# Conv-GLU behind windowed attention: the first chunk's feed-forward in float32, weights split later, and another order for the opening

## The chip, the core and the metric

The kernel runs on one core of a Trainium2 chip. The metric is the device time of one execution in microseconds (us). PE is TensorE, DVE VectorE, ACT ScalarE, POOL GpSimd, SP SyncE, whose queue issues all DMAs here.

## The reference

Eight batches of 576 positions, eight heads of 64, float32; the weights arrive as float64 (512 x 1024, 3 x 1024, 1024 x 512).

```python
scores = q @ k.T / sqrt(64)
scores = where((rel >= 0) & (rel < 128), scores - slopes[h] * abs(rel), -1e9)   # rel = query - key
attn = exp(scores - max(scores)); attn = attn / (sum(attn) + 1e-9)
x = (attn @ v)                                  # heads side by side: (8, 576, 512)
h = maximum(x @ w_in, 0)
conv = sum(conv_w[k] * h shifted by k - 1, k = 0, 1, 2)     # along positions, zero outside a batch
out = (h * sigmoid(conv)) @ w_out
```

## The kernel before

The 4608 tokens are taken in 36 tiles of 128, numbered t, and in 18 chunks of two tiles. A step s is one chunk and one pair of the eight 128-wide feature blocks f; four steps make a chunk.

Attention, for each tile and each half u of four heads: q and k are loaded (`LD`), transposed on PE (`Q`, L272) and copied out by ACT (`QO`, L276). `S` (L303) multiplies them into two PSUM banks, a = 0 and 1, each with two heads. Only 128 columns of a tile's window are live for each row: the merge `MA` puts the part of the previous tile into place with a predicated copy (L321) and then writes -1/8 of the scores plus the bias to SBUF (L334). `RM` takes the minimum (L338), `X` is exp on ACT, one instruction a head, with the row sum accumulated (L343), `N` adds 1e-9, takes reciprocals and scales on DVE (L354 to L356), `T` transposes on PE (L363), `RL` copies out on ACT (L368), `SEL` splits the two tiles' parts on GpSimd (L374, L377), and `AV` multiplies with v in float32 (L393). Scores of tiles below 9 are one float32 pass; later ones are three float32r passes on high and low parts.

The feed-forward works on high and low parts in float32r. `XH` (L404) rounds x on ACT into `ring`, `XL` (L408) subtracts on DVE. `UH` (L440) makes one feature block from 12 matmuls: four of 128 rows deep, three products each (high by high, high by low, low by high). `HH` is Relu on ACT, `Z` and `CV` the convolution (ACT into PSUM, then DVE, L472), `TH` tanh, `GT` the gate (L485), `GH` (ACT, L495) and `GL` (GpSimd, L500) its high and low part, `D` the down-projection (L517, again three products), `OB` the store. The first chunk's up-projections have 258 columns, later ones 256.

The weights come in 16 blocks of 128 x 512 doubles and one of conv weights, through six staging buffers: fetch `F` (SP), clamp `CL` (GpSimd), rebias `RS` (ACT), sign `SG` (GpSimd) or shift `SH` (DVE), bits `V` (two DVE passes, L181 and L188). `H` rounds the high half on ACT (L195). For the low half, `P` subtracts on PE: identity times the float32 weight (L206), then minus identity times the high half (L207), and `W` copies it out on ACT (L216); blocks 6, 14, 15, 16 are subtracted on DVE and block 9 on GpSimd instead (L214).

The order of all engines' instructions is written out by hand: `OPENING` for tiles 0 to 5 and steps 0 to 5, then `PERIOD` once for each tile from `FIRST` = 6 on, with its two steps, then `TAIL`. Each engine takes its instructions in that order. Names in it are as above, followed by tile, half and part, or by the step; a piece whose condition doesn't hold (a tile's `XF`, say) issues nothing. PSUM has five banks with the tag `tr` (transposes, scores, AV, up-projections), one for the convolution and two with the tag `o` for the output.

Of the kernel before, what the change touches and what calls it, by code (L numbers as in the profile page):

```python
# [646 lines left out]
```

## Time and profile before

| | |
|---|---|
| median of 3 runs | 650.45 us (648.82 to 651.15) |
| profiled execution, its own time | 651.56 us |
| its span, first to last instruction | 649.8 us |
| PE, PE weight loads | 628.3 us (97%), 551.2 us (85%) |
| DVE, ACT, GpSimd | 548.7 us (84%), 434.8 us (67%), 211.3 us (33%) |

Busy times are of one profiled execution. Matmuls overlap and their ends are modelled, so PE's busy time includes latency; a float32 matmul that is no transpose appears as two records. On DVE and ACT a record can end after the next has begun: what an instruction costs its engine is the step from its start to the next start.

### The profile page before, as it was taken

To read this page: it belongs to the slowest core of one execution; us is meant where nothing else is said; L and a number is where in the kernel's file an instruction comes from. 1 tells how busy PE (TensorE), PEld (TensorE's weight loads), DVE (VectorE), ACT (ScalarE), POOL (GpSimd) and SP (SyncE) were. 2 spreads that over 40 slices of the span, in tenths; PEclk is the share of its full clock that TensorE was granted. 3 is DMA by queue.
4 is the path that set the end of the run, shared out by engine and by line. 5 is a ranking of instruction groups with operands and counts; after the bars stand their busy time and mean duration, and the time that the engine had idled before them with its cause. 6 is when DMAs were issued, how large, how long until landed. Compare 5 with 4: busy or idle time off the path is not lost.

```text
span 649.8 us, 13737 instructions
## 1 busy us (share of the span) xinstructions
PE 628.3 (97%) x5082; PEld 551.2 (85%) x5082; DVE 548.7 (84%) x1227; ACT 434.8 (67%) x1204; POOL 211.3 (33%) x321
## 2 busy tenths in 40 slices
PE   5789999999999999999999999999999999999997
PEld 4358788888999899998899999999899989998985
DVE  6979997788888899898888898889888889899553
ACT  4868786666766576767676667666676657666653
POOL 3244633332232333333233332222223223333321
PEclk9889999999999999999999999999999999999999
DMA  8876043232323222222402232323232323000001
GB/s 242 220 187 177 21 97 82 50 83 49 83 49 83 49 67 45 74 40 73 96 34 50 65 66 51 80 49 82 50 82 49 83 49 83 18 34 1 33 16 50
DMA packets 120102, 47.04 MB, mean 72 GB/s; under 512 B 113356, under 2 KB 113380, under 8 KB 120036
## 3 DMA queue, kind: packets, MB, share of 16 engines
q1 hardware_dynamic: 120036, 46.17, 29.3%
q8 instruction: 40, 0.66, 0.4%
q14 instruction: 26, 0.21, 0.1%
HBM read 36.72 MB, written 9.44 MB: 71 GB/s over the span
## 4 chain that ended last, share of the span: by engine, by line
PE 83%; DVE 13%; issue 2%; DMA 1%; ACT 1%; POOL 0%; SPq 0%; DVEq 0%; ACTq 0%; POOLq 0%
PE p L440 30%; PE o L517 29%; PE av L393 8%; PE sc L303 8%; PE pt L272 4%; PE pa L363 4%; DVE zp L472 2%; DVE sc L321 2%; DVE wg L188 1%; DVE e L334 1%; DVE wst L181 1%; DVE st L338 1%; DVE ring L408 1%; DVE e L356 1%; DVE z L485 1%
## 5 line engine op out<-in xcount | busy, mean ns | idle before, releaser
L440 PE MATMUL p<-ring,wi 128*128 128x256 f32 (+1 forms) x1728 | 220.8, 284 | 1.5 <-DVE ring L413 1.1
L440 PEld LDWEIGHTS p<-ring,wi 128*128 128x128 f32 x1728 | 211.9, 189 | 7.6 <-PE o L517 2.4
L472 DVE SCALAR_TENSOR_TENSOR zp<-hh,cw,zp 128x256 f32<-128x256 f32 (+7 forms) x384 | 161.9, 422 | 33.5 <-ACT zp L459 22.6
L517 PE MATMUL o<-wo,gh 128*128 128x512 f32 x576 | 186.5, 404 | 0.0
L343 ACT ACTIVATE e<-e,st 128x128 f32<-128x128 f32 x288 | 112.3, 392 | 97.3 <-DVE st L338 97.3
L500 POOL TENSOR_TENSOR gl<-z,gh 128x512 fp32r<-128x512 f32 x71 | 91.3, 1286 | 193.8 <-ACT gh L495 172.8
L517 PEld LDWEIGHTS o<-wo,gh 128*128 128x128 f32 x576 | 103.2, 188 | 25.9 <-issue 5.0
L517 PE MATMUL o<-wo,gl 128*128 128x512 f32 x288 | 114.1, 396 | 0.3 <-POOL gl L500 0.3
L374 POOL TENSOR_SCALAR_AFFINE_SELECT rl<-rl 128x512 f32<-128x512 f32 x64 | 41.4, 646 | 169.9 <-ACT rl L368 166.5
L459 ACT ACTIVATE zp<-hh,cw 128x256 f32<-128x256 f32 x144 | 68.9, 479 | 20.4 <-DVE z L485 14.8
L485 DVE SCALAR_TENSOR_TENSOR z<-zp,hh 128x512 f32<-128x512 f32 (+1 forms) x73 | 49.8, 683 | 36.2 <-ACT zp L480 35.2
L480 ACT ACTIVATE zp<-zp 128x512 f32<-128x512 f32 (+1 forms) x73 | 42.3, 579 | 42.8 <-DVE zp L472 40.0
L393 PE MATMUL av<-rl,rv 128*64 128x128 f32 x1088 | 67.2, 276 | 1.2 <-PE pa L363 0.7
L517 PEld LDWEIGHTS o<-wo,gl 128*128 128x128 f32 x288 | 54.1, 188 | 13.5 <-POOL gl L500 0.7
L334 DVE SCALAR_TENSOR_TENSOR e<-sc,bias 128x256 f32<-128x256 f32 x144 | 61.2, 425 | 5.1
L393 PEld LDWEIGHTS av<-rl,rv 128*64 128x64 f32 x1088 | 58.7, 137 | 6.9 <-issue 2.8
L303 PE MATMUL sc<-qkT 64*128 64x256 f32 (+1 forms) x360 | 55.2, 357 | 1.4 <-DVE e L334 1.2
L321 DVE COPY_PREDICATED sc<-m_prev,sc 128x256 f32<-128x256 uint8 x128 | 53.8, 420 | 2.7 <-PE sc L303 2.7
L377 POOL TENSOR_SCALAR_AFFINE_SELECT rl<-rl 128x512 f32<-128x512 f32 x72 | 45.7, 635 | 30.2 <-ACT rl L368 24.6
L343 ACT ACTIVATION_READ_ACCUMULATOR e<-e,st 128x1 f32 x288 | 54.1, 188 | 0.0
L356 DVE TENSOR_TENSOR e<-e,st 128x512 f32<-128x512 f32 x72 | 50.7, 704 | 2.5
L338 DVE TENSOR_REDUCE st<-e 128x4 f32<-128x512 f32 x72 | 49.2, 685 | 2.1
(76 smaller groups left out, 745.4 us busy)
## 6 DMA issues: line engine op xcount, KB each, us to landing
out_dram<-ob SPq DMA_DIRECT2D x36, 256.0 KB, 2.2
rqk<-in_q_dram SPq DMA_DIRECT2D x32, 256.0 KB, 4.1
rqk<-in_k_dram SPq DMA_DIRECT2D x32, 256.0 KB, 4.3
rv<-in_v_dram SPq DMA_DIRECT2D x32, 256.0 KB, 3.3
wst<-in_moe_w_in_dram SPq DMA_DIRECT2D x8, 512.0 KB, 6.1
wst<-in_moe_w_out_dram SPq DMA_DIRECT2D x8, 512.0 KB, 4.1
rqk<-in_q_dram SPq DMA_DIRECT2D x8, 128.0 KB, 3.6
rqk<-in_k_dram SPq DMA_DIRECT2D x8, 128.0 KB, 3.4
```

The lines of the kernel that those rows point to most:

```text
L303: nc.tensor.matmul(to, tq[rows, slot, u, 0, g, :], of, start=n == 0, stop=n == len(passes) - 1)
L321: nc.vector.copy_predicated(out=s_cur, mask=mask.unsqueeze(1).to_broadcast(shp), data=data)
L334: nc.vector.scalar_tensor_tensor(out=heads, in0=s_cur, scalar=-0.125, in1=b, op0=ALU.mult, op1=ALU.add)
L343: nc.scalar.activation(out=e[:, j, :], in_=e[:, j, :], func=AF.Exp, bias=st[:, 0, j : j + 1], scale=-1.0, accum_out=st[:, 1, j : j + 1],)
L356: nc.vector.tensor_tensor(out=e, in0=e, in1=st[:, 2, :].unsqueeze(2).to_broadcast([P, HU, P]), op=ALU.mult)
L393: nc.tensor.matmul(ps[a * D : (a + 1) * D, u * NG + g], vraw[tt][:, u * HU + j], rl[:, side, j], start=n == 0, stop=n == len(sides) - 1,)
L440: nc.tensor.matmul(ps, a[:, cc, f * P : (f + 1) * P], ring[:, i, cc, cols], start=n == 0, stop=n == last)
L459: nc.scalar.activation(out=zps[s][:, ff, :], in_=hhs[s][:, ff, 1 : 1 + CW], func=AF.Copy, scale=cw[:, 1, f : f + 1])
L472: nc.vector.scalar_tensor_tensor(out=z[:, ff, a:cut], in0=hh[:, ff, a + kk : cut + kk], scalar=cw[:, kk, f : f + 1], in1=z[:, ff, a:cut], ...
L485: nc.vector.scalar_tensor_tensor(out=zgs[s][:, ff], in0=zps[s][:, ff], scalar=1.0, in1=hhs[s][:, ff, 1 : 1 + CW], op0=ALU.add, op1=ALU.mult,)
L500: nc.gpsimd.tensor_tensor(out=gl, in0=zgs.pop(s), in1=as32(gh), op=ALU.subtract)
L517: nc.tensor.matmul(oos[c][m], g[:, ff, ms], w[:, f, :], start=f == 0 and n == 0, stop=f == NFC - 1 and n == 2)
```

## The change

- The first chunk's up- and down-projections (steps 0 to 3) are float32, one product a matmul, on the float32 weights (`wgs`) and on `x_first`, an unsplit copy of x; they have no `GH`, and `GL` only moves the convolution's two border columns. `XL` of tiles 0 and 1 falls away.
- The low halves of all weights are subtracted on GpSimd (11 blocks) or DVE (5), written later in the order; `P` remains for the conv weights alone. The float32 weights and the low halves share 18 buffers. Seven rebias passes go to GpSimd (`RP`). Five blocks more are taken with a shift on DVE instead of a sign pass on GpSimd.
- For tiles 0 to 5 (`EARLY`), q is scaled by -1/8 in `QV`, the bias is added on PE by one float32r matmul with the identity for each bank, the merge only places and masks, the minimum is taken per bank from PSUM, and exp reads PSUM. Tiles 0 to 2 put the scores of half 0 into the output's banks. Reciprocals are taken for a tile at once (`NR`). Ten of these twelve halves are scaled on ACT (`NA`, four instructions), two on DVE.
- `OPENING` is a new order. It holds tiles 0 to 7 and steps 0 to 9, loads tile 0 in halves (`LH`), and `FIRST` is 8. `PERIOD` and `TAIL` are as before.

```diff
-    wst, wgs, pws = {}, {}, {}
-    SIGNS = {0, 1, 2, 3, 5, 6, 7, 8, 9, 10, 11, 12, 13, 14, 15, 16}
-    LOW_POOL = {9}
-    LOW_DVE = {6, 14, 15, 16}
+    wst, wgs, pws, wls = {}, {}, {}, {}
+    NWL = 18
+    SIGNS = {0, 1, 2, 8, 9, 10, 11, 12, 13, 15, 16}
+    LOW_POOL = {0, 1, 5, 6, 7, 8, 9, 13, 14, 15, 16}
...
-    def w_rebias(b):
-        g = wpool.tile([P, WB], U32, name=f"wg{b}", tag="wg")
-        wgs[b] = g[:NW, :P] if blocks[b] is None else g
-        nc.scalar.activation(out=wgs[b].bitcast(F32), in_=wst[b][..., 1].bitcast(F32), func=AF.Copy, scale=2.0**-112)
-
+    def w_rebias(b, pool=False):
+        if b in wgs:
+            pass
+        elif blocks[b] is None:
+            wgs[b] = cpool.tile([P, P], U32, name="wgc")[:NW]
+        else:
+            wgs[b] = wpool.tile([P, WB], U32, name=f"wg{b}", tag="wl", bufs=NWL)
+        g, hf = wgs[b].bitcast(F32), wst[b][..., 1].bitcast(F32)
+        if pool:
+            nc.gpsimd.tensor_scalar(out=g, in0=hf, scalar1=2.0**-112, scalar2=1.0, op0=ALU.mult, op1=ALU.mult)
+        else:
+            nc.scalar.activation(out=g, in_=hf, func=AF.Copy, scale=2.0**-112)
...
     def w_rest(b):
+        ps = pws[b] = pst.tile([P, NW], F32, name="pcw", tag="tr")
+        nc.tensor.transpose(ps, wgs[b].bitcast(F32), ident[:NW, :NW])
+
+    def w_lo(b):
         f = wgs[b].bitcast(F32)
         if blocks[b] is None:
-            ps = pws[b] = pst.tile([P, NW], F32, name="pcw", tag="tr")
-            nc.tensor.transpose(ps, f, ident[:NW, :NW])
+            nc.scalar.copy(out=cw.rearrange("p k f -> p (k f)"), in_=pws.pop(b))
             return
-        if b in LOW_POOL or b in LOW_DVE:
-            return
-        ps = pws[b] = pst.tile([P, WB], F32, name=f"pw{b}", tag="tr")
-        nc.tensor.matmul(ps, ident, f, start=True, stop=False)
-        nc.tensor.matmul(ps, nident, blocks[b][1][0], start=False, stop=True)
-
-    def w_lo(b):
-        out = cw.rearrange("p k f -> p (k f)") if blocks[b] is None else blocks[b][1][1]
-        f = wgs.pop(b).bitcast(F32)
-        if b in LOW_POOL or b in LOW_DVE:
-            eng = nc.gpsimd if b in LOW_POOL else nc.vector
-            eng.tensor_tensor(out=out, in0=f, in1=as32(blocks[b][1][0]), op=ALU.subtract)
-        else:
-            nc.scalar.copy(out=out, in_=pws.pop(b))
-
-
-
+        wls[b] = wpool.tile([P, WB], F32R, name=f"wl{b}", tag="wl", bufs=NWL)
+        eng = nc.gpsimd if b in LOW_POOL else nc.vector
+        eng.tensor_tensor(out=wls[b], in0=f, in1=as32(blocks[b][1]), op=ALU.subtract)
...
+    def load_half(t, u):
+        if t not in raws:
+            raws[t] = [apool.tile([P, 2, H, D], F32, name=f"rqk{t}", tag="rqk", bufs=3)]
+        heads = slice(u * HU, (u + 1) * HU)
+        for i, src in enumerate((q, k)):
+            fetch(t, raws[t][0][:, i, heads], src[:, heads])
...
-        nc.scalar.copy(out=qkT_of(t)[:, t % SLOTS, u], in_=pts.pop((t, u)) if t < SPLIT else pts[t, u])
+        to = qkT_of(t)[:, t % SLOTS, u]
+        if t < EARLY:
+            ps = pts.pop((t, u))
+            nc.scalar.activation(out=to[:, 0], in_=ps[:, 0], func=AF.Copy, scale=-0.125)
+            nc.scalar.copy(out=to[:, 1], in_=ps[:, 1])
+        else:
+            nc.scalar.copy(out=to, in_=pts.pop((t, u)) if t < SPLIT else pts[t, u])
...
-        pss = [pst.tile([P, NG, 2, P], F32, name=f"sc{t}_{u}_{a}", tag="tr") for a in range(2)]
+        if t < 3 and u == 0:
+            pss = [pso.tile([P, NG, 2, P], F32, name=f"sc{t}_{u}_{a}", tag="o") for a in range(2)]
+        else:
+            pss = [pst.tile([P, NG, 2, P], F32, name=f"sc{t}_{u}_{a}", tag="tr") for a in range(2)]
+        if t < EARLY:
+            for a in range(2):
+                b = heads_of(bias_r[:, u * HU : (u + 1) * HU], a)
+                to = pss[a] if first else pss[a][:, :, cur]
+                b = b.unsqueeze(2).to_broadcast([P, NG, 2, P]) if first else b
+                nc.tensor.matmul(to, ident_r, b, start=True, stop=False)
...
-                        to, tq[rows, slot, u, 0, g, :], of, start=n == 0, stop=n == len(passes) - 1
+                        to, tq[rows, slot, u, 0, g, :], of, start=n == 0 and t >= EARLY,
+                        stop=n == len(passes) - 1 and (t >= EARLY or g == NG - 1),
...
-        negb = neg.unsqueeze(2).to_broadcast(shp)
+        negb = (pos if t < EARLY else neg).unsqueeze(2).to_broadcast(shp)
...
+        if t < EARLY:
+            return
...
-    def rowmax(t, u):
+    def rowmax(t, u, a=None):
         e, st, pss = sms[t, u]
+        if t < EARLY:
+            cur = window(t)[-1]
+            least = st[:, 0].rearrange("p (g a) -> p a g", a=2)[:, a]
+            nc.vector.tensor_reduce(out=least, in_=pss[a][:, :, cur, :], axis=mybir.AxisListType.X, op=ALU.min)
+            return
         nc.vector.tensor_reduce(out=st[:, 0, :], in_=e, axis=mybir.AxisListType.X, op=ALU.min)
...
-                in_=e[:, j, :],
+                in_=pss[j % 2][:, j // 2, cur, :] if t < EARLY else e[:, j, :],
...
+    def recips(t, u=None):
+        st = sts.pop(t) if t < EARLY else sms[t, u][1]
         nc.vector.tensor_scalar(out=st[:, 2, :], in0=st[:, 1, :], scalar1=1e-9, scalar2=None, op0=ALU.add)
         nc.vector.reciprocal(out=st[:, 2, :], in_=st[:, 2, :])
+
+    def normal(t, u):
...
+    def normal_act(t, u):
+        e, st, pss = sms[t, u]
+        for j in range(HU):
+            nc.scalar.activation(out=e[:, j, :], in_=e[:, j, :], func=AF.Copy, scale=st[:, 2, j : j + 1])
         es[t, u] = e
...
+        if t < CT:
+            nc.scalar.copy(out=x_first[:, :, 1 + t * P : 1 + (t + 1) * P], in_=avs.pop(t)[0])
+            return
+        if t == CT:
+            nc.scalar.copy(out=x_first[:, :, 1 + CW : 2 + CW], in_=ps[:, :, 0:1])
...
     def x_lo(t):
+        if t < CT:
+            return
...
+            b, part = in_block(cc, f)
+            if s < NFP:
                 nc.tensor.matmul(
-                    ps, a[:, cc, f * P : (f + 1) * P], ring[:, i, cc, cols], start=n == 0, stop=n == last
+                    ps, wgs[b].bitcast(F32)[:, part], x_first[:, cc], start=cc == 0, stop=cc == NCC - 1
                 )
-                n += 1
+                continue
+            for n, (a, i) in enumerate(((blocks[b][1], 0), (blocks[b][1], 1), (wls[b], 0))):
+                nc.tensor.matmul(
+                    ps, a[:, part], ring[:, i, cc, cols], start=cc == 0 and n == 0, stop=cc == NCC - 1 and n == 2
+                )
...
+            if s < NFP:
+                zgs[s] = fpool.tile([P, 2, CW], F32, name=f"z{s}", tag="gh", bufs=3)
...
     def g_hi(s, ff=slice(0, 2)):
+        if s < NFP:
+            return
...
     def g_lo(s, ff=None):
+        if s < NFP:
+            nc.gpsimd.tensor_copy(out=hhs[s][:, :, 0:2], in_=hhs[s][:, :, CW : CW + 2])
+            return
...
+            b = out_block(f)
+            if s < NFP:
                 nc.tensor.matmul(
-                    oos[c][m], g[:, ff, ms], w[:, f, :], start=f == 0 and n == 0, stop=f == NFC - 1 and n == 2
+                    oos[c][m], g[:, ff, ms], wgs[b].bitcast(F32), start=f == 0, stop=f == NFC - 1
+                )
+                continue
+            for n, (a, w) in enumerate(((gh, blocks[b][1]), (gh, wls[b]), (gl, blocks[b][1]))):
+                nc.tensor.matmul(
...
     OPENING = """
-    LD0 Q0 F1 QO0 S0.0 CL1 RS1 S0.1 MA0.0.0 MA0.1.1 LD1 F2 SG1 Q1 MA0.1.0 V1 QO1 S1.0 F0 MA0.0.1 MA1.0.1 LD2
-    CL2 CL0 RM0.0 S1.1 RS2 RS0 F7 H1 F3 X0.0.0 SG2 F5 X0.0.1 MA1.1.1 SG0 LV0 Q2 MA1.0.0 F4 P1 QO2 V0 F9
-    RM0.1 S2.1 F8 N0.0 LD3 W1 X0.1.1 V2 MA1.1.0 MA2.1.1 T0.0 X0.1.0 RL0.0 H0 SEL0.0 P0 RM1.1 H2 S2.0 W0 CL3
...
+    LH0.1 QU0.1 QV0.1 LH0.0 QU0.0 QV0.0 LD1 F4 S0.1 F2 CL4 MA0.1.0 CL2 RM0.1.0 S0.0 RS4 XF3 QU1.1 MA0.0.1
+    MA0.1.1 QU1.0 X0.1.0 MA0.0.0 QV1.1 RP2 RM0.0.0 LD2 F5 RM0.1.1 SG2 RM0.0.1 S1.1 F6 GH0 MA1.1.0 CL5 F0
+    QU2.1 V2 QU2.0 CL6 QV1.0 LD3 RM1.1.0 X0.0.0 F1 MA1.1.1 X0.0.1 RM1.1.1 S1.0 X0.1.1 QV2.1 X1.1.0 NR0 N0.0
+    GH2 F7 MA1.0.1 S2.1 RP6 LD4 RM1.0.1 MA2.1.0 QV2.0 MA1.0.0 X1.1.1 NA0.1 X1.0.1 RM1.0.0 RM2.1.0 T0.0 LV0
+    X1.0.0 SH4 CL0 T0.1 V4 NR1 S2.0 RL0.1 QU3.0 MA2.1.1 F3 N1.0 SH5 SEL0.1 RM2.1.1 X2.1.0 QL7 MA2.0.0 NA1.1
+    RL0.0 RM2.0.0 CL1 XF0 OB4 QU3.1 QV3.0 MA2.0.1 RP0 LD5 S3.0 RM2.0.1 MA3.0.1 RP1 CL7 SG0 QV3.1 SH7 F8 LV1
+    T1.1 X2.1.1 MA3.0.0 RM3.0.1 S3.1 MA3.1.0 LV2 P4 X2.0.0 RL1.1 RM3.0.0 X2.0.1 X3.0.1 MA3.1.1 RS7 RP5 T1.0
...
+    D0 XH4 H8 Z2.0 W1 H11 W0 T5.1 GT1 GL0 W3 OB5 LV6 QV7.0 SG12 S7.0 XL4 HH2.1 RS16 NA5.0 W7 HH3.1 RL5.1 XL3
+    XF2 XF4 S7.1 W2 CV2.0 RM6.0 MA7.0.0 Z2.1 T5.0 UH4.0 W8 UH4.1 X6.0.0 H9 CV2.1 RP13 TH2 UH5.0 GL1 MA7.1.0
...
-    FIRST = 6
+    FIRST = 8
```

## Rows read from the trace of the kernel before

**Rows 1.** The page: PE's busy tenths in 40 slices of the span

```profile
PE   5789999999999999999999999999999999999997
```

**Rows 2.** Windows: us, busy PE, loads, DVE, ACT, POOL; clock, DMA share, GB/s

```profile
0.00:55.56 55.56, 40.92 (x259) 26.99 (x259) 45.42 (x114) 37.23 (x107) 20.74 (x39) 0.91 0.79 209
8.37:55.56 47.19, 37.53 (x243) 24.30 (x241) 42.23 (x93) 34.78 (x104) 19.19 (x30) 0.89 0.80 214
55.56:135.23 79.67, 78.14 (x589) 67.08 (x587) 69.24 (x140) 59.19 (x161) 33.86 (x49) 1.00 0.31 73
```

**Rows 3.** Chain that ended last, 100 to 136 us: start, us, what, records

```profile
101.07 1.93 PE sc L303 x16
103.00 1.90 PE av L393 x32
...
107.89 4.29 PE p L440 x36
112.17 0.87 PE pt L272 x8
...
114.91 2.80 PE o L517 x12
...
135.23 0.84 PE sc L303 x5
```

**Rows 4.** The same chain from 0 to 120 us

```profile
1.30 4.30 DMA rqk<-in_k_dram
...
18.61 0.09 DVE st L354
18.72 0.19 DVE st L355
18.93 0.69 DVE e L356
...
20.95 0.35 DVE sc L321
21.32 0.42 DVE e L334
...
22.61 0.59 DVE st L338
...
38.66 0.93 PE pw L206 x2
39.58 0.23 PE pw L207
```

**Rows 5.** Timeline of ACT: start, us, line, instruction

```profile
59.90 0.38 ACT L449 ACTIVATE hh<-p 128x258 f32<-128x258 f32 x1
60.18 0.39 ACT L343 ACTIVATE e<-e,st 128x128 f32<-128x128 f32 x1
60.47 0.19 ACT L343 ACTIVATION_READ_ACCUMULATOR e<-e,st 128x1 f32 x1
60.56 0.39 ACT L343 ACTIVATE e<-e,st 128x128 f32<-128x128 f32 x1
...
60.95 0.57 ACT L368 COPY rl<-pa 128x512 f32<-128x512 f32 x1
61.41 0.67 ACT L166 ACTIVATE wg<-wst 128x512 f32<-128x512 f32 x1
```

**Rows 6.** Groups on GpSimd, first 115 us: count | busy us, mean ns | idle

```profile
L500 POOL TENSOR_TENSOR gl<-z,gh 128x512 fp32r<-128x512 f32 x6 | 7.9, 1316 | 14.0 <-ACT gh L495 11.4 <-DVE wo L214 2.6
...
L214 POOL TENSOR_TENSOR wo<-wg,wo 128x512 fp32r<-128x512 f32 x1 | 1.7, 1723 | 0.0
```

**Rows 7.** Timeline of GpSimd and DVE at 51.7 us

```profile
51.69 0.68 POOL L171 TENSOR_SCALAR wst<-wst 128x512 f32<-128x512 f32 x1
51.87 1.04 DVE L356 TENSOR_TENSOR e<-e,st 128x512 f32<-128x512 f32 x1
```

**Rows 8.** The page, costliest groups: weight loads of the up-projection

```profile
L440 PEld LDWEIGHTS p<-ring,wi 128*128 128x128 f32 x1728 | 211.9, 189 | 7.6 <-PE o L517 2.4
```

More of the change, by code (lines that the diff above doesn't have):

```diff
@@ L70, in tile_alibi_window_attention_conv_glu @@
     nc.vector.memset(neg, NEG)
+    pos = cpool.tile([P, 1], F32, name="pos")
+    nc.vector.memset(pos, -0.125 * NEG)
     def mask_from(name, conds):
@@ L107, in tile_alibi_window_attention_conv_glu @@
     )
-    bias = cpool.tile([P, H, P], F32, name="bias")
+    EARLY = 6
+    bias_r = cpool.tile([P, H, P], F32R, name="bias")
+    bias = as32(bias_r)
     for h in range(H):
@@ L111, in tile_alibi_window_attention_conv_glu @@
         nc.vector.tensor_scalar(
-            out=bias[:, h, :], in0=dist, scalar1=slope, scalar2=None, op0=ALU.mult
+            out=bias_r[:, h, :], in0=dist, scalar1=slope, scalar2=None, op0=ALU.mult
         )
-    wi = [cpool.tile([P, NCC, DFF], F32R, name=f"wi{i}") for i in range(2)]
-    wo = [cpool.tile([P, NFC, DM], F32R, name=f"wo{i}") for i in range(2)]
+    wi = cpool.tile([P, NCC, DFF], F32R, name="wi")
+    wo = cpool.tile([P, NFC, DM], F32R, name="wo")
     cw = cpool.tile([P, 3, NFC], F32, name="cw")
@@ L131, in weight_blocks @@
             for c in range(NCC):
-                yield moe_w_in[c * P : (c + 1) * P, cols], [w[:, c, cols] for w in wi]
+                yield moe_w_in[c * P : (c + 1) * P, cols], wi[:, c, cols]
             if part == 0:
@@ L135, in weight_blocks @@
         for f in range(NFC):
-            yield moe_w_out[f * P : (f + 1) * P, :], [w[:, f, :] for w in wo]
+            yield moe_w_out[f * P : (f + 1) * P, :], wo[:, f, :]
     wpool = ctx.enter_context(tc.tile_pool(name="wpool", bufs=3))
@@ L235, in tile_alibi_window_attention_conv_glu @@
     ring = cpool.tile([P, 2, NCC, RING + 4], F32R, name="ring")
-    nc.vector.memset(as32(ring[:, :, :, 2:3]), 0.0)
+    x_first = cpool.tile([P, NCC, XW], F32, name="x_first")
+    nc.vector.memset(x_first[:, :, 0:1], 0.0)
     def window_x(c):
-        if c == 0:
-            return slice(2, 2 + XW)
         a = 4 + c * CW % RING
@@ L312, in merge @@
             e = apool.tile([P, HU, P], F32, name=f"e{t}_{u}", tag="e", bufs=4)
-            st = apool.tile([P, 3, HU], F32, name=f"st{t}_{u}", tag="st", bufs=5)
+            if t >= EARLY:
+                st = apool.tile([P, 3, HU], F32, name=f"st{t}_{u}", tag="st", bufs=5)
+            else:
+                if t not in sts:
+                    sts[t] = apool.tile([P, 3, H], F32, name=f"st{t}", tag="sts", bufs=2)
+                st = sts[t][:, :, u * HU : (u + 1) * HU]
             sms[t, u] = e, st, sms[t, u]
@@ L431, in up @@
             ps = pts[s, ff, "up"] = pst.tile([P, 512], F32, name=f"p{s}_{ff}", tag="tr")
-            ps = ps[:, : cols.stop - cols.start]
+            ps = ps[:, : XW if s < NFP else CW]
         else:
@@ L483, in gate @@
         if s not in zgs:
-            zgs[s] = fpool.tile([P, 2, CW], F32, name=f"z{s}", tag="z", bufs=2)
+            if s < NFP:
+                zgs[s] = fpool.tile([P, 2, CW], F32, name=f"z{s}", tag="gh", bufs=3)
+            else:
+                zgs[s] = fpool.tile([P, 2, CW], F32, name=f"z{s}", tag="z", bufs=2)
         nc.vector.scalar_tensor_tensor(
@@ L515, in down @@
             ms = slice(m * P, (m + 1) * P)
-            for n, (g, w) in enumerate(((gh, wo[0]), (gh, wo[1]), (gl, wo[0]))):
+            b = out_block(f)
+            if s < NFP:
                 nc.tensor.matmul(
-                    oos[c][m], g[:, ff, ms], w[:, f, :], start=f == 0 and n == 0, stop=f == NFC - 1 and n == 2
+                    oos[c][m], g[:, ff, ms], wgs[b].bitcast(F32), start=f == 0, stop=f == NFC - 1
[3 more added lines that the diff above has]
+                nc.tensor.matmul(
+                    oos[c][m], a[:, ff, ms], w, start=f == 0 and n == 0, stop=f == NFC - 1 and n == 2
                 )
@@ L549, in tile_alibi_window_attention_conv_glu @@
     TILE = {
-        "LD": load, "LV": loadv, "Q": qk, "QO": qk_out, "QL": qk_rest, "S": scores, "MA": merge, "RM": rowmax,
-        "X": lambda t, u, h: exps(t, u, range(2 * h, 2 * h + 2)),
-        "N": normal, "T": attnT, "RL": attn_out, "SEL": select, "AV": av, "XH": x_hi, "XL": x_lo, "XF": xfin,
+        "LD": load, "LH": load_half, "QU": qkT, "QV": qkT_out, "LV": loadv, "Q": qk, "QO": qk_out, "QL": qk_rest, "S": scores, "MA": merge, "RM": rowmax,
+        "X": lambda t, u, h: exps(t, u, range(h, HU, 2) if t < EARLY else range(2 * h, 2 * h + 2)),
+        "NR": recips, "N": normal, "NA": normal_act, "T": attnT, "RL": attn_out, "SEL": select, "AV": av, "XH": x_hi, "XL": x_lo, "XF": xfin,
     }
@@ L596, in tile_alibi_window_attention_conv_glu @@
+    V16 GH4 RL7.0 LD9 AV5 SEL6.1 SEL7.0 CV5.1 GH1 TH5 GT5 H12 AV6 XH6 D3 XH5 W9 HH6 W12 GH5 XL5 Z6.0 XL6 H13
+    UH8.0 CV6.0 Z6.1 CV6.1 OB3 H14 TH6 GL5 Z7.0 GT6 GL4 UH9.0 W13 CV7.0 XL1 OB6 W10 H16 UH8.1 X7.1.1 W11 GH6
+    Z7.1 N7.1 LV7 GL6 W16 D4 W14 CV7.1 TH7 HH8 Z8.0 H4 GT7 LD10 GH7 CV8.0 D5 Z8.1 D6 UH9.1 GL7 HH9 CV8.1 TH8
+    T7.1 W15 GT8 Z9.0 RL7.1 SEL7.1 LV8 GH8 GL8 D7 CV9.0 Z9.1 OB7 CV9.1 TH9 GT9
     """
```

63 lines of the change are left out of this document (35 added, 28 removed).

## Prediction

> **What bounds the kernel now.** Read the 40 slices first: TensorE (PE) is busy nine tenths or more from the fourth of them on, less in the first three [rows 1]. But a busy PE is not a dense one. The chain that ended last says where PE sets the time: from 101.07 us on it is PE, instruction behind instruction, two tiles in the 34.16 us to 135.23 [rows 3]. Before that the chain runs through VectorE (DVE) [rows 4]. [...] So a change to the opening is worth what it brings forward in PE's work, and nothing after it is changed: at 135.23 PE starts the scores of tile 8, the same instructions follow in both programs, with Q8, AV6, D7 and UH9 issued before it in both. I forecast the start of tile 8's scores, T8.
>
> **PE's own work up to T8.** Costs are steps from start to start. From [rows 3]: an up unit (12 float32r matmuls of 256 columns) 4.29 / 3 = 1.43; a down unit (12 of 512) 2.80; AV 1.90; eight transposes 0.87; a float32 score half of four matmuls 0.97 (half of 1.93). From [rows 4]: a float32 matmul of 512 columns, written as two records, 0.93; the float32r one behind it 0.23. In the order before, up to tile 8: nine transposed tiles 7.8, 16 halves of scores 14.5 (tile 0 at half price), 11 weight splits of 0.93 + 0.23 = 12.8, one of 0.2 for the conv weights, 16 probability transposes 7.0, AV 12.4 (tile 0 half), 20 up units 28.6, 8 down units 22.4: 105.7 of 135.2. Thirty us are lost, 26 of them before the first up-projection (30.0 of work in 55.56).
>
> The change takes the 11 splits away (-12.8). It adds 20 bias matmuls of 512 columns and 4 of 256: 20 x 0.233 + 4 x 0.119 = +5.1. A float32 up unit is 4 matmuls at four times 0.119: 1.91, eight of them +3.8. A float32 down unit is 4 x 0.93 = 3.72, four of them +3.7. Sum -0.2: PE's work stays 105.5. [...]
>
> **DVE**, 45.4 + 69.2 = 114.7 busy to T8 [rows 2]. Merge without bias: -24 x 0.42 = -10.1; ten scalings go to ACT: -10 x 0.69 = -6.9; reciprocals for a tile at once: -6 x (0.11 + 0.21) = -1.9; 12 minima over 512 (0.59) become 24 over 256 from PSUM, 0.30 to 0.42, taken at 0.38 (near the 0.35 to 0.42 of a PSUM pass of that width): +2.0; two fewer remainders of x: -1.4 [all rows 4]. Five shifts more, not in the trace at that width: above 0.35 (a pass of half the width), at most 0.69, taken at 0.4 as they have one input: +2.0; one low half more: +0.7. Sum -15.6: 99.
>
> **ACT**, 37.2 + 59.2 = 96.4 [rows 2]. An instruction is followed by the next some 0.1 before it ends [rows 5]. Gone: 11 copies of low halves (0.47), 7 rebias passes (0.67 less 0.1), 4 roundings of the gate (0.5): -5.2 - 4.0 - 2.0. New: 40 scalings of 128 columns. The exp of that shape steps 0.29 before its accumulator read; a 258-column Relu steps 0.28, so a plain one may be 0.19. I take 0.29, the same shape with a pointer operand: +11.6 (low end +7.6). Copies of q and k in two halves of 256 columns, 0.28 each for 0.48: 12 x 0.08 = +1.0. Sum +1.4: 98. The exps now read PSUM, at the same price here. [...]
>
> **GpSimd**, 54.6 [rows 2]: ten subtractions more at 1.32 to 1.72 [rows 6], +15; 7 rebias passes and 5 fewer sign passes at 0.68 [rows 7], +1.4; four fewer gate remainders, -5.3: 66. Not the bound.
>
> **DMA.** Same bytes; the weights still go through six buffers, and SyncE's (SP) queue holds tile 4's and 5's loads behind weights 7 and 3, which wait for a staging buffer that a DVE pass on an earlier weight frees; both are among DVE's first 12 us of work, and those tiles' transposes are over 25 us in. The opening's first transfers, half the heads of q and k, are half of the bytes that had landed by 5.60 [rows 4]; the first transposes move up by about a us, and I put ACT's first copy at 4.5.
>
> **Waits that are added.** Sixteen weights and their low halves share 18 buffers, so the third low half waits for a weight that the first chunk has done with. Behind it on DVE stand the second chunk's passes, on GpSimd the selections of tile 5; the up-projections that free the buffer stand ahead of the waiting passes by 5 us and more of PE's work, so I cost it at nothing; if that cover is gone, the second chunk's first up-projection is late by what is missing. The wait for score banks is rival 3.
>
> **First stage, to the first up-projection.** Written ahead of it in the new order: on ACT 12 copies of q and k halves (6.7), 4 rebias passes (2.0), 40 exps at 0.39 (15.6), 24 scalings (7.0), 8 copies of probabilities (3.9), x (1.7): 37.0. On DVE, 3.2 of constants and 20 merges (10.1), 20 minima (7.6), seven weights (8.7), the rest 5.6: 35.2 instead of 45.4. On PE 28.0: 12 half transposes 5.2, 11 halves of scores 9.7 and their bias 4.7, 8 probability transposes 3.5, AV 4.8, 0.2. So ACT leads where DVE led. From 4.5, 37.0 at the 89% at which DVE worked gives 46. Its floor is 41.5; with the low price for the scalings, 43. I take 45.5, since part of the doubt is on that side; up to 52 if three engines of nearly the same load wait for each other.
>
> **Second stage.** PE has 105.5 - 28.0 = 77.5 left, ACT 61, DVE 64. Before, PE lost 3.9 here (75.8 of work in 79.7). With DVE lighter I take 3, between 1 and 8. T8 = 45.5 + 77.5 + 3 = 126.0 against 135.23: 9.2 us earlier. The profiled execution took 651.56, which is 1.1 above the median of the runs: 642.4, and for a median **641**.
>
> **Rivals.**
> (1) *The engines interlock nearly without waiting.* ACT at its floor, 41.5, and 1 lost afterwards: T8 = 120, **635**. For it: four engines have slack. Against it: with ACT 37, DVE 35 and PE 28 at a clock that was 0.89 [rows 2] no engine clearly leads, and each wait is passed on.
> (2) *GpSimd blocks DVE.* In [rows 7] a DVE multiply of two SBUF tensors took 1.04 instead of 0.69 because a GpSimd pass of 0.68 had begun 0.18 before it. Ten subtractions of 1.32 or more, nearly all after the first up-projection, could each hold such a DVE pass (weights, scaling, remainders) for their whole length: 13 us, DVE 77 of some 80, at 89% that is 86. T8 = 45.5 + 86 = 132, **647**. Against it: most DVE work of that stage, conv, has one operand in PSUM. [...]
> (3) *No change: PSUM banks.* Exps read the scores where they lie, so a half of scores holds two banks until its last exp, not until its merge: at least 1.4 + 4 x 0.38 + 4 x 0.39 = 4.5 us against some 2.6. Five banks also serve transposes; the first three tiles borrow the output's two. The eight other halves before the up-projection, two at a time, take 48 us once a half holds its banks for 12. From the first scores at 6 the first stage then ends at about 55: T8 = 135.5, **651**.
> (4) *Slower: float32 matmuls that show their weight loads.* One load is 0.189 [rows 8]; 48 float32 matmuls have two each. If none were hidden, +18: T8 = 144, **659**. The gain is gone once half of them show. Against it: AV is float32 with two loads a matmul, and its 32 records run back to back at 59 ns [rows 3].
>
> **Chances and range.** Forecast 0.52, (1) 0.17, (2) 0.15, (3) 0.10, (4) 0.06. A difference under 0.5% can hardly be told from none; faster than 647.2 are the forecast but for 0.03, all of (1) and half of (2): 0.74; same 0.17 (the other half, most of (3), the 0.03); slower 0.09. The range 631 to 650 leaves out (4), two thirds of (3) and the far end of (1).
>
> **What would show it.** First up-projection near 45 us with ACT at nine tenths ahead of it; T8 near 126; no L206; up records in the first chunk at twice the columns, a float32 unit near 1.9, a down unit near 3.7; the row minimum near 0.38 and ACT's scaling near 0.29 a step; all after T8 as before. Wrong if the opening's PE rows wait on exps for banks, if DVE passes beside GpSimd subtractions stretch past a microsecond in number, or if a later stage changes.

## The result, and the profile after

The changed kernel takes 639.77 us (median of four runs, 638.63 to 640.18). The kernel before, run beside it, took 650.2, and the ratio is 0.9838, 95% interval 0.9816 to 0.9861. The prediction was 641, range 631 to 650. The profiled execution took 639.5 us with a span of 637.4.

The windows of the changed kernel, cut at the first up-projection and at the start of tile 8's scores (us, busy PE, loads, DVE, ACT, POOL, granted clock, DMA share, GB/s), answer to [rows 2]:

```profile
0.00:46.13 46.13, 38.75 (x272) 26.08 (x273) 35.58 (x98) 36.93 (x145) 21.13 (x36) 0.96 0.98 235
46.13:125.04 78.91, 77.14 (x516) 61.09 (x515) 66.72 (x128) 57.14 (x154) 46.68 (x59) 1.00 0.34 84
125.04:637.40 512.36, 506.58 (x4241) 456.68 (x4240) 433.43 (x973) 337.91 (x938) 157.12 (x234) 1.00 0.25 58
```

The span is 12.4 us shorter. Of that, 9.43 lies ahead of the first up-projection (55.56 before, 46.13 now), 0.76 between there and tile 8's scores (79.67, now 78.91), and 2.21 behind them, where both programs are the same: 649.80 - 135.23 = 514.57 before, 512.36 now. ACT and DVE have nearly the same work in the first stage, the DMA share there is 0.98 where it was 0.79, and the mean granted clock 0.96 where it was 0.91. The 12.4 is the difference of two single executions; the medians differ by 10.4, since the profiled execution of the kernel before was slower than its median and the changed kernel's was not.

The page's busy tenths for PE [rows 1 has them before]:

```profile
PE   7899999999999999999999999999999999999997
```

PE is below nine tenths in the first two slices, where it was in the first three.

The chain that ended last, from the first up-projection to tile 8's scores (start, us, what, records), answers to [rows 3]:

```profile
46.13 1.76 PE p L505 x8
...
87.21 3.44 PE o L596 x8
...
119.53 1.29 POOL gl L577
...
120.95 1.24 POOL wl L217
...
122.23 2.81 PE o L601 x11
125.04 1.06 PE sc L336 x7
```

A float32 up unit (the first row) is 1.76 us and a float32 down unit 3.44. At the end of the stage TensorE waits for two GpSimd subtractions, the second of them a weight's low half.

### The profile page after: what moved, and what is told of

It is laid out like the page before. It is cut to its first block, busy times and chain, and to the rows that moved or that the text cites. A ratio compares the mean times of both kernels' runs of the same rounds, so it can differ in the third digit from the quotient of the medians.

```text
span 637.4 us, 13650 instructions
## 1 busy us (share of the span) xinstructions
PE 622.5 (98%) x5025; PEld 543.8 (85%) x5025; DVE 535.7 (84%) x1197; ACT 432.0 (68%) x1235; POOL 224.9 (35%) x329
## 4 chain that ended last, share of the span: by engine, by line
PE 77%; DVE 11%; ACT 6%; issue 2%; DMA 2%; SPq 1%; POOL 1%; DVEq 0%; ACTq 0%; POOLq 0%
PE p L510 27%; PE o L601 24%; PE av L451 8%; PE sc L336 7%; PE pa L421 4%; DVE zp L541 4%; PE pt L285 4%; DMA rqk<-in_k_dram 2%; PE p L505 1%; DVE z L557 1%; ACT e L390 1%; PE o L596 1%; DVE sc L360 1%; ACT zp L549 1%; DVE e L375 1%
## 5 line engine op out<-in xcount | busy, mean ns | idle before, releaser
L510 PE MATMUL p<-ring,wi 128*128 128x256 f32 x1088 | 200.3, 285 | 1.7 <-DVE ring L478 1.5
L510 PEld LDWEIGHTS p<-ring,wi 128*128 128x128 f32 x1088 | 168.3, 188 | 7.3 <-PE o L601 2.7
L390 ACT ACTIVATE e<-e,st 128x128 f32<-128x128 f32 x240 | 93.5, 391 | 87.5 <-DVE st L384 87.5
L510 PE MATMUL p<-ring,wl 128*128 128x256 f32 x544 | 152.5, 280 | 0.0
L601 PE MATMUL o<-wo,gh 128*128 128x512 f32 x272 | 112.4, 413 | 0.0
L601 PE MATMUL o<-wl,gh 128*128 128x512 f32 x272 | 105.8, 389 | 0.7 <-POOL wl L217 0.7
L510 PEld LDWEIGHTS p<-ring,wl 128*128 128x128 f32 x544 | 102.9, 189 | 0.0
L601 PEld LDWEIGHTS o<-wo,gh 128*128 128x128 f32 x272 | 51.1, 188 | 13.3 <-issue 4.6
L601 PEld LDWEIGHTS o<-wl,gh 128*128 128x128 f32 x272 | 51.2, 188 | 9.8 <-POOL wl L217 1.0
L375 DVE SCALAR_TENSOR_TENSOR e<-sc,bias 128x256 f32<-128x256 f32 x120 | 51.0, 425 | 4.2
```

Of the source, the lines that this page charges most:

```text
L375: nc.vector.scalar_tensor_tensor(out=heads, in0=s_cur, scalar=-0.125, in1=b, op0=ALU.mult, op1=ALU.add)
L390: nc.scalar.activation(out=e[:, j, :], in_=pss[j % 2][:, j // 2, cur, :] if t < EARLY else e[:, j, :], func=AF.Exp, bias=st[:, 0, j : j + ...
L510: nc.tensor.matmul(ps, a[:, part], ring[:, i, cc, cols], start=cc == 0 and n == 0, stop=cc == NCC - 1 and n == 2)
L601: nc.tensor.matmul(oos[c][m], a[:, ff, ms], w, start=f == 0 and n == 0, stop=f == NFC - 1 and n == 2)
```

## The experiments

Each kernel below is the changed kernel with an edit (two in e9, e10 and e12), but for the padded kernel before. e11 and e13 leave a part of the computation out. "First up" and "tile 8" are the starts of the first up-projection and of tile 8's scores in PE's timeline, whose rows begin up to 0.2 us ahead of the chain's steps. "Rest" is the span less the latter. The ratio is to runs of the kernel before on the same chip.

| kernel | us | ratio (95%) | first up | tile 8 | rest |
|---|---|---|---|---|---|
| before | 650.2 | 1 | 55.56 | 135.16 | 514.6 |
| changed | 639.77 | 0.9838 (0.9816 to 0.9861) | 45.97 | 124.97 | 512.4 |
| e1 loads first | 642.94 | 0.9874 (0.9855 to 0.9893) | 49.47 | 128.61 | 512.3 |
| e9 the same, weight 7 later | 640.89 | 0.9866 (0.9838 to 0.9893) | 45.89 | 125.96 | 512.6 |
| e2 scaling on DVE | 644.24 | 0.9891 (0.9868 to 0.9914) | 48.09 | 129.80 | 512.7 |
| e13 no scaling on ACT | 638.42 | 0.9817 (0.9781 to 0.9853) | 44.36 | 124.10 | 512.4 |
| e11 three weights unsplit | 640.16 | 0.9847 (0.9824 to 0.9870) | 46.63 | 125.60 | 512.7 |
| e3 bias on DVE | 644.42 | 0.9899 (0.9881 to 0.9916) | 50.33 | 130.48 | 512.3 |
| e7 two banks fewer | 643.74 | 0.9905 (0.9881 to 0.9928) | 49.02 | 128.25 | 512.4 |
| e4 low halves on DVE | 644.45 | 0.9901 (0.9881 to 0.9920) | 46.02 | 130.98 | 512.4 |
| e10 lows | 638.21 | 0.9820 (0.9798 to 0.9842) | 45.12 | 123.18 | 513.6 |
| e12 end | 638.51 | 0.9823 (0.9805 to 0.9842) | 45.52 | 123.89 | 512.3 |
| e5 before, padded | 648.40 | 0.9972 (0.9959 to 0.9985) | 55.32 | 133.88 | 512.6 |
| e6 changed, padded | 638.97 | 0.9833 (0.9812 to 0.9854) | 44.88 | 123.77 | 513.2 |

Five of these do the same up to the first up-projection: the changed kernel, e4, e6, e10 and e12. They start it at 44.88 to 46.02, 45.5 in the mean, so about 1.1 us there is the difference of one execution from the next, and a single kernel's shift below that says nothing.

**e1 and e9, the order of the loads.**

```diff
-... F1 ... GH2 F7 MA1.0.1 S2.1 RP6 LD4 ... RP0 LD5 S3.0
+... F1 ... GH2 LD4 LD5 F7 MA1.0.1 S2.1 RP6 ... RP0 S3.0
 e9 besides: CL7, RS7 and SH7 moved to shortly ahead of V7
```

> The loads of tiles 4 and 5 are put ahead of weight 7 in SyncE's queue, which waited 5.32 us there; nothing else moves. If the transfers and the queue in front of them limit the first stage (its DMA share is 0.98 in the changed kernel, and tile 5's transposes start 0.04 us after its k lands at 32.91), the first up-projection comes 2 to 3 us earlier, at 43 to 44 instead of 46.13, and the kernel takes 637 to 638. If ACT or DVE leads that stage, as the forecast had it with the DMA costed at nothing, the first up-projection stays within 0.5 us of 46.13 and the time at 639.8.

> The loads of tiles 4 and 5 ahead of weight 7, as in the run of that order, and weight 7's clamp, rebias and shift moved from their places in the first stage to just ahead of where its bits are joined, so that no engine waits for weight 7 early. In the run without this move DVE waited for weight 7 until 28.65 us and everything behind it was late. If that wait alone ate the gain of the earlier loads, the first up-projection now comes at 43 to 45 (46.13 in the changed kernel, 49.5 in that run). If transfers of tiles are not what the stage waits for, it stays at 46 or later. What arrives at tile 8's scores may be less than what the first stage gains, as DVE sets the second stage too: putting 7.7 us of low halves on it moved tile 8 by 6.0.

Both expectations of e1 missed: it came 3.5 us later. Its chain (start, us, what):

```profile
22.02 6.61 DMA wst<-in_moe_w_in_dram
...
28.65 0.04 DVE wst L184
...
28.99 0.42 DVE sc L360
```

Weight 7's load was issued at 22.02 and its shift on DVE could not begin until 28.65; the merge of scores at 28.99 stood behind it. In e9 that wait is gone and so is the loss, 45.89. So a weight that is late costs time because a pass on it stands in DVE's order ahead of work that is due. But no gain is left either, which misses the 43 to 45 expected of earlier loads. TensorE still waits for a transfer in both kernels, only for another one. In PE's timeline (idle time before the row in brackets) it is tile 5's k in the changed kernel,

```profile
32.95 0.87 PE L285 MATMUL pt<-ident_r,rqk 128*128 128x128 f32 x6 [0.35 <-DMA rqk<-in_k_dram]
```

and the first v in e9, whose load was issued at 25.93 instead of 20.97, behind the moved ones:

```profile
30.69 1.09 PE L451 MATMUL av<-rl,rv 128*64 128x128 f32 x16 [1.43 <-DMA rv<-in_v_dram]
```

So the loads of tiles 4 and 5 alone do not set the stage; whether the transfers together do, with the DMA share at 0.98, no run shows.

**e2, e11 and e13, DVE against ACT in the first stage.**

```diff
 e2:  -NA0.1 ... NA5.0        +N0.1 ... N5.0
 e11: w_shift, w_bits:        +if b in (5, 6, 7): return
 e13: normal_act:             -nc.scalar.activation(out=e[:, j, :], ..., scale=st[:, 2, j : j + 1])
```

> All scaling of probabilities in the first six tiles goes back to DVE, one instruction of 512 columns for four of 128 on ACT; the reciprocals stay as in the changed kernel. Ahead of the first up-projection ACT does some 7.0 us less and DVE 4.1 more. If ACT leads there, as forecast, the first up-projection comes 2 to 5 us earlier (41 to 44) and the kernel takes 635 to 638. If DVE is still what sets it, 3 to 4 us later (49 to 50), 643. If the stage is balanced or led by transfers, within 1 us of 46.13, and what changes is the second stage.

> Left out of the computation: DVE's shift and its two joining passes for weights 5, 6 and 7 (0.42 + 0.69 + 0.69 us each by the rows of the changed kernel, 5.4 in all, 4.0 of it ahead of the first up-projection), so those weights are wrong; their loads and what ACT and GpSimd do on them stay, but their staging buffers come free a little earlier. If DVE sets the opening, as the run with the scaling put back on it says (4.1 more there, 2.0 later), the first up-projection comes 2 to 3 us earlier, at 42.5 to 44, and tile 8's scores 3 to 4.5, at 120.5 to 122; some of that may be lost behind, where DVE still has a backlog. 635.5 to 638. If ACT leads, as the prediction had it, nothing comes earlier than the 44.9 to 46.1 of kernels with this opening, and 639 to 640.

> Left out of the computation: the ten scalings of probabilities that the changed kernel does on ACT (40 instructions; the two on DVE stay), so six tiles' attention is not normalised. ACT has some 7 us less ahead of the first up-projection, DVE and TensorE what they had. Taking 5.4 us from DVE alone gained nothing there, and putting the scaling on DVE made it 2 us later with DVE busy for 97% from 14 us on. If ACT is what sets the stage in the changed kernel (busy 97 to 99% from 24 us on in the run with the moves at the end), the first up-projection comes 1.5 to 4 us earlier than the 44.9 to 46.1 of kernels with this opening, at 42 to 44, with DVE (33.6 us of work from 3.2 on) next in line. If TensorE's own order sets it (38.6 us busy in that stretch), or the transfers do, it stays at 44.9 or later. How much of it reaches the end is open: DVE has the second stage.

The windows from 3.2 us to the first up-projection (columns as above), first of the changed kernel, then of e2, e11 and e13:

```profile
3.20:46.13 42.93, 38.75 (x272) 26.08 (x273) 33.76 (x86) 35.64 (x144) 19.64 (x27) 0.96 1.03 246
```

```profile
3.20:48.09 44.89, 38.59 (x272) 27.57 (x273) 37.44 (x89) 29.23 (x120) 20.14 (x28) 0.96 1.04 232
```

```profile
3.20:46.63 43.43, 40.11 (x271) 27.42 (x272) 29.47 (x79) 35.52 (x144) 17.93 (x28) 0.96 1.02 250
```

```profile
3.20:44.36 41.16, 38.20 (x271) 26.57 (x271) 33.03 (x81) 29.25 (x121) 19.33 (x27) 1.00 1.05 237
```

With the scaling on DVE, DVE is busy 37.44 of 44.89 us, ACT only 29.23, and the stage is 2 us longer, less than the 3 to 4 expected of a stage that DVE sets: it was not ACT alone that set it. Tile 8 is 4.8 later, so more than half of e2's loss lies in the second stage. With 4.3 less on DVE the stage is no shorter (43.43), a miss for the theory that DVE sets it. With 6.4 less on ACT it is 1.8 shorter than in the changed kernel. Its start of 44.36 is 1.1 below the mean of the five kernels with the same opening, but only 0.5 below the earliest, so the gain of one execution hardly leaves their spread. The time does not tell e13 from the changed kernel.

The end of the stage shows better where ACT leads. From 24 us to the first up-projection, in the changed kernel, in e12 (the same opening) and in e13:

```profile
24.00:46.13 22.13, 19.38 (x162) 13.65 (x161) 18.76 (x41) 19.90 (x77) 11.81 (x15) 0.92 1.04 240
```

```profile
24.00:45.52 21.52, 19.34 (x170) 13.48 (x170) 18.86 (x44) 21.16 (x84) 10.99 (x16) 1.00 1.03 232
```

```profile
24.00:44.36 20.36, 19.43 (x172) 13.56 (x170) 19.18 (x41) 17.11 (x70) 12.31 (x17) 1.00 1.03 211
```

ACT is busy 21.16 of 21.52 us in e12. In the execution of the changed kernel that was profiled it is 19.90 of 22.13, with the wait for tile 5's loads and a lower clock in between. With ACT relieved, PE (19.43 of 20.36) and DVE (19.18) are nearly full. So ACT leads by little: taking work from it hands the stage to the next engines, and adding work to DVE lengthens it.

**e3, the bias back on DVE.**

```diff
-            nc.tensor.matmul(to, ident_r, b, start=True, stop=False)
+            nc.vector.scalar_tensor_tensor(out=s_cur, in0=s_cur, scalar=1.0, in1=b, op0=ALU.mult, op1=ALU.add)
```

> The bias of the first six tiles goes back from TensorE to DVE: no bias matmuls (PE 4.7 us less ahead of the first up-projection), and a pass over 256 columns in PSUM for each merge (some 0.42 us, 20 of them there, DVE 8.4 more, 24 in all). If the gain of the change is the DVE work taken out of the opening, the first up-projection falls back to 51 to 54 and the start of tile 8's scores by 5 to 8 us, 645 to 648 in all. If the gain comes from elsewhere (the weight splits taken off TensorE, or half transfers), 1 us or less is lost, 640 to 641, or TensorE's 4.7 us come back as a gain.

Its window:

```profile
3.20:50.33 47.13, 36.76 (x250) 25.52 (x250) 42.25 (x103) 36.03 (x145) 18.95 (x27) 0.86 0.96 219
```

DVE now has 42.25 of 47.13 us, nine tenths, as before the change [rows 2]. The first up-projection is 4.4 us later and tile 8 5.5. That is just under the expected 51 to 54, and half of what the change brought, undone by one part of it; TensorE's 4.7 us did not come back. The granted clock is lower too, 0.86 against 0.96 (last section).

**e7, banks.**

```diff
-        if t < 3 and u == 0:
+        if False:
```

> The first halves of scores of tiles 0 to 2 no longer borrow the two PSUM banks of the output; all scores and transposes of the opening share five. Nothing else moves. If banks held until the last exp are what the first stage waits for (the third rival), two banks fewer cost it 2 us or more: first up-projection at 48 or later, 642 and up. If not, it stays between 44.9 and 46.1, where four kernels with this same opening had it, and the kernel takes 639 to 640.

The first up-projection starts at 49.02, as the third rival would have it, and PE waits for banks that ACT frees. Waits of PE in the first stage (total, times, longest), in the changed kernel

```profile
PE sc L326 <- ACT e L390: 0.6, 2, 0.4
```

and in e7:

```profile
PE sc L326 <- ACT e L390: 1.0, 2, 0.6
...
PE av L451 <- ACT e L390: 0.6, 1, 0.6
PE sc L326 <- ACT qkT L293: 0.5, 2, 0.3
```

So the third rival's mechanism is there. With seven banks these waits are 0.6 us; with five they are 2.1, and the stage is 3.5 us longer than in the mean of the five kernels. How the other 2 us come about was not followed up.

**e4, e10 and e12, the second stage.**

```diff
 e4:  -LOW_POOL = {0, 1, 5, 6, ... 16}   +LOW_POOL = {}
 e10: +2, 3 in LOW_POOL;                 W15 moved from behind T7.1 to ahead of GL7
 e12: -N7.1  +NR7.1 NA7.1;               W15 as in e10, LOW_POOL as it was
```

> The eleven low halves of weights that GpSimd subtracts go to DVE (0.7 us each, 7.7 more in all; GpSimd some 16 us less), all after the first up-projection, which stays at 46.1. If each GpSimd subtraction holds up DVE passes beside it (some 4 us of DVE time by the stretched passes in the changed kernel's trace, and the chain ends on two GpSimd subtractions), the start of tile 8's scores stays within 1 us of 125.04 or comes up to 1.5 earlier: 638.5 to 640. If DVE and GpSimd hardly disturb each other, DVE has 74.4 of 78.9 us to do and tile 8's scores come 2 to 4 us later: 642 to 644.

> Two of the low halves that DVE still makes (weights 2 and 3, some 71 to 75 us into the span) go to GpSimd, and the last one, weight 15's, which GpSimd makes behind a gate remainder with TensorE waiting for it at 122.2, is put ahead of that remainder. First stage as in the changed kernel, 46.1. If DVE sets the middle of the second stage, the first down-projection (87.21 in the changed kernel) comes 1 to 1.5 us earlier, and the moved low half takes another 1.2 off the wait ahead of tile 8's scores: 122.5 to 123.5 for them instead of 125.04, 637 to 638 in all. If GpSimd's passes hold DVE up for as long as they save, the down-projection stays at 87 and only the 1.2 remains.

> Two moves at the end of the second stage: weight 15's low half ahead of the gate remainder on GpSimd, as in the run of the lows, and the scaling of tile 7's second half from DVE (1.65 us there, stretched beside a GpSimd subtraction) to ACT, which waited 4.07 us at that place. From the first down-projection to tile 8's scores the changed kernel takes 37.9 us, the run of the lows 36.95; here 35.3 to 36. In the run of the lows 1.2 us of the gain was given back by tile 14, as TensorE then waited for DVE (remainder of x at 147.6). If DVE's work is what stands there, taking 1.65 from it lets the gain stay: 1 to 2.5 us less than the changed kernel, 637.3 to 638.8. If GpSimd and DVE hold each other up anyway, or the wait moves to ACT, 639 to 640.

Groups of DVE instructions between first up-projection and tile 8 (xcount | busy, mean ns), in the changed kernel:

```profile
L197 DVE SCALAR_TENSOR_TENSOR wg<-wg,wst 128x512 uint32<-128x512 uint32 x10 | 8.8, 884 | 0.3
L190 DVE SCALAR_TENSOR_TENSOR wst<-wst 128x512 uint32<-128x512 uint32 x8 | 6.6, 830 | 0.0
...
L408 DVE TENSOR_TENSOR e<-e,st 128x512 f32<-128x512 f32 x4 | 3.7, 932 | 0.1
...
L217 DVE TENSOR_TENSOR wl<-wg,wi 128x512 fp32r<-128x512 f32 x2 | 2.2, 1102 | 0.0
```

and in e4:

```profile
L197 DVE SCALAR_TENSOR_TENSOR wg<-wg,wst 128x512 uint32<-128x512 uint32 x10 | 7.2, 724 | 0.3
...
L190 DVE SCALAR_TENSOR_TENSOR wst<-wst 128x512 uint32<-128x512 uint32 x8 | 5.9, 742 | 0.0
...
L408 DVE TENSOR_TENSOR e<-e,st 128x512 f32<-128x512 f32 x4 | 2.8, 692 | 0.1
```

Beside GpSimd's subtractions the same shape takes 830 to 932 ns, without them 692 to 742. Still e4 lost 6.0 us, more than the expected 2 to 4 and all of it in this stage: the low halves cost DVE more than the waiting beside GpSimd does. In e10 two more of them on GpSimd gained nothing up to the second down-projection (87.21 in the chain above; the expectations call it the first, which began at 71.00): it lies 41.1 us behind the first up-projection in both, so there it made no difference which of the two engines subtracts. Weight 15's move did what was expected: 36.95 us from there to tile 8 instead of 37.92. But the rest grew by 1.2, and its chain shows why:

```profile
146.77 0.61 DVE ring L473
...
147.73 4.49 PE p L510 x36
```

The chain runs through DVE, with short pieces of ACT, up to 147 us, and TensorE's up-projection waits for DVE's remainder of x. e12 took a scaling from DVE and kept the gain (rest 512.3); as it also left weights 2 and 3 where they were, the two are not separated. From the second down-projection to tile 8 it took 36.96, not the expected 35.3 to 36. The chain says why the scaling brought nothing there: at the end of the second stage it is TensorE throughout, so nothing is left to gain from DVE:

```profile
111.08 8.26 PE o L601 x36
119.33 1.42 PE p L510 x12
120.75 0.44 PE pa L421 x4
121.19 2.77 PE o L601 x12
123.96 1.93 PE sc L336 x16
```

e12's span is 1.2 below the changed kernel's, 0.45 of it in the first stage, which it does not touch. In the times the two are not told apart (638.51 and 639.77, the intervals overlap).

**e5 and e6, where the weights lie.**

```diff
+    cpool.tile([P, 8], F32, name="pad0")
     wi = ...
     wo = ...
     cw = ...
+    cpool.tile([P, 8], F32, name="pad1")
```

> The kernel before, with 32 unused bytes put ahead of the weight tiles in SBUF and 32 behind them: the start addresses of the weights become multiples of 64 bytes (they were 32 above one), and every other tile keeps its place modulo 64. Same instructions in the same order. If the roughly 2 us that the changed kernel gains after tile 8's scores (512.36 us from there to the end, 514.57 before) come from where the weights lie, this kernel gains 1.5 to 3 us over the kernel before, spread evenly over the span, and a 512-column step of the down-projection falls by some 1.5%. If addresses do not matter, the ratio is 1.000 within 0.002 and the tail keeps its 514.6.

> The mirror of the padded kernel before: in the changed kernel the rounded weights are put 32 bytes above a multiple of 64, everything else stays modulo 64. If their place is what the tail gained by, the stretch behind tile 8's scores goes from 512.4 to some 514 us and the kernel takes 641 to 642; the low halves, which lie elsewhere, keep a part of it, so 1 to 2 us is what can be lost. If addresses do not matter, 639.8 and 512.4 as in the changed kernel.

Two down units of a tile in the steady part of the chain: before,

```profile
373.58 2.99 PE o L517 x12
...
383.58 2.80 PE o L517 x12
```

padded before,

```profile
371.37 2.95 PE o L519 x12
...
381.31 2.76 PE o L519 x12
```

changed,

```profile
362.38 2.95 PE o L601 x12
...
372.33 2.75 PE o L601 x12
```

changed with the weights put off by 32 bytes:

```profile
371.50 2.78 PE o L603 x12
...
378.23 2.99 PE o L603 x12
```

With the weights at a multiple of 64 bytes, by the sizes in the source, the units are 2.95 and 2.75 to 2.76, in both programs; off it they are 2.99 and 2.80 in the kernel before, 2.99 and 2.78 in the changed one, whose low halves stayed in place. The kernel before gains 1.8 us by 64 bytes of nothing, and its rest falls to 512.6. In the changed kernel the reverse costs 0.8 in the rest, above every other changed kernel but e10, yet under the expected 1 to 2. The time misses the expected 641 to 642 and does not show it; the profiled execution's opening was 1.1 earlier.

## Why the prediction was right, and where it was not

**The forecast point** held: 126.0 for tile 8, measured 125.04, from a first up-projection at 45.5, measured 46.13 (mean of the five, 45.5).

**"ACT leads where DVE led"** is right late in the stage, and by little. DVE's 35.2 us were measured at 35.58. ACT's 37.0 were 35.64, from its first copy at 4.67 on; the 36.93 in the windows also hold a record of 1.28 us at 0.80 (`ACT_TABLE_LOAD`), which the sum did not have. From that copy to the first up-projection ACT was busy 86% (35.64 of 41.46 us) where 89% was put (DVE's 42.23 of 47.19 [rows 2]). e12's end of the stage, ACT busy 98% from 24 us on, bears out that it leads, and e13 shows by how little: 6.4 us taken from it returned some 1 us. That a lead is not clear was in the forecast's own words against the first rival; the floor of 41.5 was never near.

**TensorE.** The float32 units were put at 1.91 and 3.72 and are 1.76 and 3.44. Over 4 x 258 and 4 x 512 columns that is 1.71 and 1.68 ns a column, where the forecast had 1.85 and 1.82. 8 x 0.15 + 4 x 0.28 = 2.3 us too much. The second stage, put at 77.5 + 3, took 78.91; with this correction TensorE lost 3.7 there. The bias matmuls were sized rightly (two of 512 in 0.47).

**DVE** was to fall to 99 and fell to 102.3. The rows above give the size: 10 x 0.19 + 8 x 0.14 + 4 x 0.24 + 2 x 0.41 = 4.8 us over the 0.69 that these passes take undisturbed. Not all of it is due to the subtractions: the first three groups are 3.2 us shorter in e4, which has none on GpSimd. That is rival (2), with its mechanism and a quarter to a third of its price of 13, which took every subtraction to hold a pass for its whole length. Single passes do show it, here a scaling beside two GpSimd subtractions:

```profile
114.19 2.99 POOL L217 TENSOR_TENSOR wl<-wg,wo 128x512 fp32r<-128x512 f32 x2
```

```profile
114.37 1.65 DVE L408 TENSOR_TENSOR e<-e,st 128x512 f32<-128x512 f32 x1
```

The scaling took 1.65 us instead of 0.69; the sum shows that most of the subtractions' length met no such pass. The convolution's passes of 256 columns, with one operand in PSUM, were no longer for it: 486 ns in the changed kernel, 487 in e4.

**ACT**, 98 forecast, 94.1 measured. Exps of one shape read PSUM in the opening and SBUF from tile 6 on; in ACT's timeline of the changed kernel (start, us, line, instruction), against [rows 5]:

```profile
17.71 0.39 ACT L390 ACTIVATE e<-sc,st 128x128 f32<-128x128 f32 x1
...
18.05 0.39 ACT L390 ACTIVATE e<-sc,st 128x128 f32<-128x128 f32 x1
...
111.15 0.40 ACT L390 ACTIVATE e<-e,st 128x128 f32<-128x128 f32 x1
...
111.54 0.39 ACT L390 ACTIVATE e<-e,st 128x128 f32<-128x128 f32 x1
```

The durations are alike, the steps are not: 0.34 from PSUM, 0.39 from SBUF, 48 x 0.05 = 2.4 us of the 3.9. I had put them at the same price. The scaling was sized rightly (four in 1.16 to 1.17 us, 0.29 each).

**DMA at nothing** is not borne out. Moving tiles 4 and 5 gained nothing (e9), but TensorE does wait for tile 5, against the cover that the prediction saw, and e1 shows 3.5 us between two orders of the same queue, by way of a weight.

**Waits for banks** cost 0.6 us by PE's waits in the first stage, as forecast little; e7 shows that there was no margin of two banks. The low halves' wait for buffers, costed at nothing, is not seen: no engine stood idle ahead of one. Rival (4) falls by the float32 units.

**"All after tile 8 as before"** is the step that failed, by 2.2 us. The instructions are the same, but the weights lie elsewhere. The change takes out a negative identity and a second copy of each weight, whose sizes are multiples of 64 bytes, and adds a constant of one column, `pos`, beside `neg`, ahead of the weights. That it is `pos` that moves their start against 64 is an estimate from the sizes in the source; no run shows the addresses themselves. e5 shows that the place of the weights (with that of the small conv weights, which moved along) gives 2.0 of the 2.2 in the kernel before. In the changed kernel e6 takes back only 0.8, with the low halves left in place, so in that kernel it is shown in part. Without it the result would have been near 642, one above the forecast. Up to tile 8 the change brings 10.2 us in the two profiled executions and, by the medians, 10.4 - 2.2 = 8.2; the forecast's 9.2 lies between. So 641 is right in its mechanism, with the first stage worth what was said, but that the median comes this near is luck: an unforeseen gain in the rest is about as large as the errors in the terms.

Open: whether TensorE alone would set the first stage with ACT and DVE both lighter; what the transfers together cost there; what the half loads, the splits taken off TensorE and the float32 chunk each bring, as none was taken back alone; and why the padded kernel before reaches tile 8 1.3 us earlier, since executions differ by that much.

## What to carry to other kernels

Ask of a stage with three engines near the same load what the second busiest has, not only the first: here 6 us less on the leader gave some 1 us, and moving that work to the next one cost 2. A wait taken away from one engine gained nothing here where another had a backlog behind it (e10: 0.97 us won ahead of tile 8, 1.2 lost behind it), so follow the chain past the place of the gain. When tiles are added or removed, compare the addresses of the operands that TensorE streams before reading a difference of a few tenths of a per cent as a matter of scheduling: e5 made one of 0.28% by 64 bytes of padding.

## What the runs showed of the hardware that was not expected

The start address of a down-projection's weights, 32 bytes off a multiple of 64 by the sizes in the source, cost 1 to 1.5% of a unit of 12 matmuls of 512 columns: 2.99 against 2.95 us and 2.80 against 2.76 in the kernel before, 2.99 against 2.95 and 2.78 against 2.75 in the changed one.

The granted clock of TensorE fell behind a stretch in which it had nothing to do. In e3 (columns as above):

```profile
16.00:18.00 2.00, 0.00 (x0) 0.00 (x0) 1.90 (x6) 2.00 (x11) 1.75 (x3) 1.00 1.24 285
```

```profile
20.00:28.00 8.00, 7.00 (x24) 4.42 (x24) 7.65 (x21) 6.16 (x27) 5.05 (x8) 0.50 1.17 255
```

PE is idle from 16 to 18 us, and from 20 to 28 the clock is 0.50. In the changed kernel, with the bias matmuls, PE is busy 9.35 of 10 us from 14 on and the clock is 1.00:

```profile
14.00:24.00 10.00, 9.35 (x56) 5.57 (x54) 8.88 (x26) 9.37 (x43) 5.29 (x8) 1.00 1.06 258
```

So the bias on TensorE may have paid twice; that the idle stretch brought the clock down is an estimate from these rows, and how much of e3's loss is the clock was not measured. The changed kernel has a dip of its own, 0.51 between 36 and 39 us, behind 6.09 busy of 8 us; e10, e12 and e13 have none before the first up-projection.
